# First pair's operands in a fixed order, and weights handled in pairs of blocks

## The chip, the core and the metric

The kernel runs on one core of one Trainium2 chip, as one program. The metric is device time in microseconds, the median of several runs. One execution more is taken by the hardware profiler; the views below are of that one. Engines are named as the profile names them: PE is TensorE (PEld its weight loads), DVE VectorE, ACT ScalarE, POOL GpSimd, SP the SyncE queue, which issues every DMA of this kernel.

## The reference

```python
q_bits = (einsum('bhsd,dk->bhsk', q, proj) > 0)          # 6 hash bits; k_bits likewise
mask = q_bucket[:, :, :, None] == k_bucket[:, :, None, :]
scores = where(mask, q @ k.T / sqrt(D), -1e9)
attn = exp(scores - max); attn = attn / (sum(attn) + 1e-9)
x = (attn @ v), heads side by side                       # [1536, 512]
h = maximum(x @ w_in1, 0); x = h * h @ w_out1
h = x @ w_in2; out = (maximum(h, 0) + alpha * minimum(h, 0)) @ w_out2
```

Batch 2, 8 heads, 768 positions, 64 columns a head; the feed-forward layers have 2048 hidden columns. Weights arrive as 64-bit floats and lie in memory as their bits, so the kernel itself has to turn them into 32-bit floats.

## The kernel before

**Tiling.** The 1536 rows are cut into four chunks of 384 (half a batch entry each). A chunk's attention goes by four pairs of heads (`Pair`), each pair with 2 x 3 score tiles of 128 x 768. A chunk's feed-forward pass goes by 16 blocks of 128 hidden columns: `hidden` multiplies x with a block of w_in, `project` the activated block with a block of w_out; the projection runs one block behind. Two layers of four chunks make eight passes of 16 blocks.

**Precision.** Every matmul operand is split into a high and a low half, both of the rounded type fp32r, and products are summed from several matmuls. For scores the halves, and rows that encode the hash ids, are stacked in 128 rows: q1 and k1, q2 and k2. So each pair has to be prepared: hash bits (`hash_bits`: a small matmul, then a sign on DVE), a match matmul with a constant code (`matches`), high and low halves, and id rows. For all pairs but the first, halves and id rows are computed for both heads in one instruction and moved to their place by DMA (`k_split`, `k_ids`, `q_split`, `q_ids`: 14 moves a pair, all on SP). The first pair computes its pieces in place, each head for itself; its queries come by a load of their own (`qr`).

**Weights.** `load_bits` loads a block's bits (512 KB), `to_f32` converts it (one ACT copy with a scale into the tile `we`, three DVE operations with the scratch tile `wsg`), `ahead` and `fetch` store the float block to memory for later passes (256 KB), and `split_w` makes the high half on ACT and the low half on POOL or DVE. All of it is done block by block, 512 columns an instruction. In passes 1 and 2 of the first layer the second layer's 32 blocks are converted beside the other work (`conversion`, a load and a conversion for each block as two steps).

**Order.** Chunk 0's attention runs alone. Then each feed-forward pass of the first layer carries the next chunk's attention in its slots: a `Background` runs the attention's steps by marks in time. A planner in the language's layer orders the instructions of each engine by priority and its own picture of time, except for instructions given to `keep_in_program_order`, which stay in the order of the program among themselves. In the kernel before these are the constants on DVE (L150 to L168) and the first pair's two sign instructions (L235). Every engine works its list strictly in order, and SP its DMA issues too. `prepare` gives the steps of a pair's preparation; one of them is put behind each score tile of the pair before, from its second tile on, and the raw loads of the next pair are the last step (`ahead`).

**Buffers.** Raw keys and queries have two buffers (`p2`); before the handover a weight block has four buffers (`whole`), its bits three (`wide`), its halves two; `we` and `wsg` have one each.

## Time and profile before

| | us |
|---|---|
| median of 3 runs | 852.25 (851.3 to 853.84) |
| the profiled execution | 850.58 |
| its span, first to last instruction | 848.8 |
| first matmul of the first feed-forward pass | 86.49 |

| engine | busy us | share of the span |
|---|---|---|
| PE | 798.8 | 94% |
| PEld | 648.0 | 76% |
| DVE | 504.0 | 59% |
| ACT | 470.5 | 55% |
| POOL | 359.6 | 42% |

A busy time is the union of an engine's instructions in the profile. Matmuls overlap and their ends are modelled, so a busy PE may still have small holes. A wait is put down to the instruction whose semaphore came last. The idle time of an engine that nobody waits for costs nothing.

### The profile page before, as it was taken

Reading aid. Unit: us, or ns where it says so; the run is one execution under the profiler, and the core shown is the slowest. Engines: PE = TensorE matmul, PEld = TensorE weight load, DVE = VectorE, ACT = ScalarE, POOL = GpSimd, SP = SyncE. Lnnn points to the kernel's source line nnn. Section 1 sums busy time; section 2 is a strip of 40 time slices with the busy share of each in tenths; the row PEclk is TensorE's granted clock in tenths of the full one; section 3 lists DMA queues with packets and bytes.
Section 4 is the critical chain, followed back from the end, with each engine's and each line's share of the span. In section 5 each row is a group of like instructions: output and inputs, shape, how many; then the busy total and the mean of one; then the engine's idle time right before and its main releaser. Section 6 shows DMA issues by size and latency. Waiting matters only on the chain.

```text
span 848.8 us, 12785 instructions
## 1 busy us (share of the span) xinstructions
PE 798.8 (94%) x4384; PEld 648.0 (76%) x4384; DVE 504.0 (59%) x819; ACT 470.5 (55%) x919; POOL 359.6 (42%) x315
## 2 busy tenths in 40 slices
PE   3988799999999989999989999999999999999997
PEld 1656486767787666677677789989989998998996
DVE  6576789998567567788888431224435445444442
ACT  3566587777575655565565556654434443444332
POOL 1000232323555565533333355545555555555553
PEclk9999799999999999999999999999999999999999
DMA  7567767777867767778775489600101011000001
GB/s 206 153 174 214 226 229 249 239 252 249 228 215 215 236 192 240 234 245 257 241 219 170 120 310 314 233 29 10 38 1 37 1 38 38 1 1 37 1 1 38
DMA packets 62096, 130.09 MB, mean 153 GB/s; under 512 B 8816, under 2 KB 21072, under 8 KB 62032
## 3 DMA queue, kind: packets, MB, share of 16 engines
q1 hardware_dynamic: 62032, 129.28, 48.6%
q8 instruction: 35, 0.57, 0.3%
q14 instruction: 29, 0.24, 0.1%
HBM read 83.32 MB, written 23.12 MB: 125 GB/s over the span
## 4 chain that ended last, share of the span: by engine, by line
PE 48%; DVE 7%; DMA 3%; issue 2%; ACT 2%; POOL 1%; SPq 0%; POOLq 0%; DVEq 0%; ACTq 0%
PE acc L608 7%; PE acc L604 7%; PE acc L605 7%; PE m L578 4%; PE m L576 4%; PE m L577 4%; PE h L576 3%; PE h L577 3%; PE h L578 3%; PE m L387 3%; DMA w<-we 2%; DVE low L354 1%; DVE wsg L504 1%; DVE we L507 1%; DVE pt L377 1%
## 5 line engine op out<-in xcount | busy, mean ns | idle before, releaser
L594 POOL TENSOR_TENSOR gl<-g,gh 128x384 fp32r<-128x384 f32 x128 | 136.1, 1063 | 246.0 <-ACT gh L593 123.2
L604 PE MATMUL acc<-wh,gh 128*128 128x512 f32 x384 | 158.2, 412 | 0.0
L529 POOL TENSOR_TENSOR wl<-wf,wh 128x512 fp32r<-128x512 f32 x80 | 108.4, 1356 | 112.8 <-ACT wh L528 102.5
L605 PE MATMUL acc<-wl,gh 128*128 128x512 f32 x384 | 152.1, 396 | 0.0
L528 ACT ACTIVATE wh<-w 128x512 fp32r<-128x512 f32 x128 | 80.5, 629 | 80.8 <-PE m L577 45.6
L608 PE MATMUL acc<-wh,gl 128*128 128x512 f32 x384 | 115.8, 398 | 2.1 <-POOL gl L594 2.1
L528 ACT ACTIVATE wh<-wf 128x512 fp32r<-128x512 f32 x128 | 80.5, 630 | 64.8 <-PE h L577 24.2
L576 PE MATMUL h<-xh,wh 128*128 128x384 f32 x296 | 106.7, 360 | 4.6 <-ACT xh L415 3.2
L354 DVE TENSOR_REDUCE low<-s 128x1 f32<-128x768 f32 x84 | 80.1, 953 | 38.0 <-PE s L351 37.8
L577 PE MATMUL h<-xl,wh 128*128 128x384 f32 x296 | 101.6, 343 | 0.4 <-POOL xl L416 0.4
L578 PE MATMUL h<-xh,wl 128*128 128x384 f32 x296 | 101.5, 343 | 0.0
L357 ACT ACTIVATE sm<-s,low 128x768 f32<-128x768 f32 x84 | 75.6, 900 | 37.5 <-DVE low L354 37.1
L608 PEld LDWEIGHTS acc<-wh,gl 128*128 128x128 f32 x384 | 71.5, 188 | 21.3 <-POOL gl L594 5.0
L371 PE MATMUL m<-ident,sm 128*128 128x128 f32 x525 | 82.9, 276 | 4.0 <-ACT sm L357 1.8
L529 POOL TENSOR_TENSOR wl<-w,wh 128x512 fp32r<-128x512 f32 x64 | 82.7, 1291 | 6.0 <-ACT wh L528 6.0
L604 PEld LDWEIGHTS acc<-wh,gh 128*128 128x128 f32 x384 | 72.4, 189 | 15.9 <-issue 5.7
L605 PEld LDWEIGHTS acc<-wl,gh 128*128 128x128 f32 x384 | 72.5, 189 | 9.2 <-issue 0.6
L593 ACT ACTIVATE gh<-g 128x384 fp32r<-128x384 f32 x64 | 33.5, 524 | 81.7 <-DVE g L592 81.7
L591 DVE TENSOR_SCALAR r<-m,alpha_sb 128x384 f32<-128x384 f32 x43 | 26.6, 618 | 87.0 <-PE m L578 86.7
L371 PEld LDWEIGHTS m<-ident,sm 128*128 128x128 f32 x525 | 64.1, 141 | 18.5 <-ACT sm L357 3.0
L350 PE MATMUL s<-k,q 128*128 128x384 f32 x168 | 63.9, 380 | 12.6 <-ACT sm L357 10.6
L578 PE MATMUL m<-xh,wl 128*128 128x384 f32 x216 | 73.0, 338 | 0.5 <-DVE wl L529 0.5
(112 smaller groups left out, 1475.2 us busy)
## 6 DMA issues: line engine op xcount, KB each, us to landing
wf<-w SPq DMA_DIRECT2D x96, 256.0 KB
wbits<-in_w_in_dram SPq DMA_DIRECT2D x32, 512.0 KB
wbits<-in_w_out_dram SPq DMA_DIRECT2D x32, 512.0 KB
w<-wf SPq DMA_DIRECT2D x32, 256.0 KB
w<-we SPq DMA_DIRECT2D x32, 256.0 KB
w<-w SPq DMA_DIRECT2D x32, 256.0 KB
q<-qh SPq DMA_DIRECT2D x60, 96.0 KB
k<-kh SPq DMA_DIRECT2D x28, 192.0 KB
```

The costliest lines, as they stand in the source:

```text
L354: nc.vector.tensor_reduce(low, ps[:, 0:2, 0:HALF], AX.XY, ALU.max, negate=True)
L357: nc.scalar.activation(sm.rearrange("p (a n) -> p a n", a=2), ps[:, 0:2, 0:HALF], AF.Exp, bias=low, accum_out=self.sums[:, i:i + 1],)
L371: nc.tensor.transpose(ps[:, i * P:(i + 1) * P], pp[:, b * P:(b + 1) * P], ident)
L528: nc.scalar.activation(hi, w, AF.Copy)
L529: engine.tensor_tensor(lo, w, f32(hi), ALU.subtract)
L576: nc.tensor.matmul(hp, wih[:, ks], xh[:, kk, :], start=first, stop=False)
L577: nc.tensor.matmul(hp, wih[:, ks], xl[:, kk, :], start=False, stop=False)
L578: nc.tensor.matmul(hp, wil[:, ks], xh[:, kk, :], start=False, stop=last)
L594: nc.gpsimd.tensor_tensor(gl, g, f32(gh), ALU.subtract)
L604: nc.tensor.matmul(acc[:, t, :], gh[:, blocks[t]], woh, start=first, stop=False)
L605: nc.tensor.matmul(acc[:, t, :], gh[:, blocks[t]], wol, start=False, stop=False)
L608: nc.tensor.matmul(acc[:, t, :], gl[:, blocks[t]], woh, start=False, stop=last)
```

## The change

The first pair gets a routine of its own, `at_once`, in which the DVE operations, the hash matmuls and signs stand in a written order (`self.next` is `keep_in_program_order` for the first two pairs of chunk 0). Two of its pieces are copied by POOL and two moved by DMA; the extra load `qr` goes. A pair's raw loads are issued by the first preparation step of the pair before, across chunks too, and in chunk 0 two preparation steps stand behind a score tile, from the first tile on. The low half of the queries is written over the raw ones.

A block of w_out and the next block of w_in are now a unit: one tile of 2 x 512 columns is loaded, converted, stored, fetched and split together, with one ACT instruction of 1024 columns for the high half and three DVE instructions of 1024 columns for a conversion. The ACT step of the conversion writes over the bits, and the tile `we` is gone: what `ahead` converts is left in `wsg` and stored from there. Low halves stay one instruction a block. `split(i)` stands once at the head of block i (before: w_in of block i + 1 and w_out of block i as two splits), `fetch` reaches one block ahead (before: two). `whole` and `wide` have two buffers of a pair each before the handover, eight after it. The rest of the diff saves a few small tiles among the constants.

```diff
+        def next(self, ins):
+            if self.c == 0 and self.j < 2:
+                tc.keep_in_program_order(ins)
...
+        def at_once(self):
+            self.start()
+            self.new_k()
+            self.new_q()
+            r = [self.rows(h)[0] for h in range(2)]
+            o = [self.rows(h)[1] for h in range(2)]
+            k_bits = self.hash_bits(self.kr, S)
+            for h in range(2):
+                nc.scalar.activation(self.k1[r[h], h], self.kr[r[h]], AF.Copy)
+            for h in range(2):
+                nc.scalar.activation(self.q1[r[h], h], self.qn[r[h]], AF.Copy, scale=scale)
+            nc.gpsimd.tensor_copy(self.k2[r[0], 0], f32(self.k1[r[0], 0]))
+            nc.gpsimd.tensor_copy(self.q1[o[0], 0], f32(self.q1[r[0], 0]))
+            nc.sync.dma_start(out=f32(self.k2[r[1], 1]), in_=f32(self.k1[r[1], 1]))
+            nc.sync.dma_start(out=f32(self.q1[o[1], 1]), in_=f32(self.q1[r[1], 1]))
+            k_y = self.matches(k_bits, S)
+            for h in range(2):
+                self.next(nc.vector.tensor_tensor(
+                    self.k1[o[h], h], self.kr[r[h]], f32(self.k1[r[h], h]), ALU.subtract
+                ))
+                if h == 0:
+                    q_y = self.matches(self.hash_bits(self.qn, T), T)
+                    for g in range(2):
+                        nc.scalar.activation(self.q2[o[g], g], q_y[o[g], 0, :], AF.Relu, bias=off[o[g]])
+                self.next(nc.vector.tensor_scalar(
+                    self.k2[o[h], h].rearrange("p (a n) -> p a n", n=T), k_y[o[h]], pop[o[h]], NEG,
+                    ALU.not_equal, ALU.mult,
+                ))
+                self.next(nc.vector.scalar_tensor_tensor(
+                    self.q2[r[h], h], self.qn[r[h]], scale, f32(self.q1[r[h], h]), ALU.mult, ALU.subtract
+                ))
...
             def ahead():
-                if self.j + 1 < NPAIR:
-                    load_pair(self.c, self.j + 1)
+                c, j = divmod(self.c * NPAIR + self.j + 1, NPAIR)
+                if c < NCH:
+                    load_pair(c, j)
             def first():
+                ahead()
                 self.start()
...
+            if self.first:
+                return [self.at_once, ahead]
+            if self.c % 2:
+                return [first, self.q_ids]
+            return [first, self.k_split, self.k_ids, self.q_split, self.q_ids]
...
-                if nxt and u > 0:
-                    steps.append(nxt.pop(0))
+                for _ in range(2 if c == 0 else 1):
+                    if nxt:
+                        steps.append(nxt.pop(0))
...
+    def to_f32(us, w=None):
+        if us not in w_bits:
+            load_bits(us)
+        n = len(us)
+        t = w_bits.pop(us)
+        e = t[:, 0:n, :, 1]
+        nc.scalar.activation(e.bitcast(F32), e.bitcast(F32), AF.Copy, scale=2.0 ** -112)
+        s = state["conv"].tile([P, 2, DM], U32, tag="wsg", name="wsg")[:, 0:n]
+        nc.vector.tensor_scalar(s, e, 0x80000000, None, ALU.bitwise_and)
+        nc.vector.scalar_tensor_tensor(s, t[:, 0:n, :, 0], 29, s, ALU.logical_shift_right, ALU.bitwise_or)
+        w = s if w is None else w.bitcast(U32)
+        nc.vector.scalar_tensor_tensor(w, e, 3, s, ALU.logical_shift_left, ALU.bitwise_or)
+        return w.bitcast(F32)
+
+    def ahead(us):
+        store(us, to_f32(us))
...
+    def blocks_of(i):
+        u = []
+        if 0 <= i:
+            u.append((work[i][0], work[i][2], 1))
+        if i + 1 < len(work):
+            u.append((work[i + 1][0], work[i + 1][2], 0))
+        return tuple(u)
...
+    def split(i):
+        us = blocks_of(i)
+        w, parts = w_f.pop(i)
+        hi = state["parts"].tile([P, 2, DM], F32R, tag="wh", name="wh")
+        lo = state["parts"].tile([P, 2, DM], F32R, tag="wl", name="wl")
+        if parts is None:
+            nc.scalar.activation(hi, w, AF.Copy)
+            parts = [w[:, 0], w[:, 1]]
+        else:
+            for k, p in enumerate(parts):
+                nc.scalar.activation(hi[:, k], p, AF.Copy)
+        for k, u in reversed(list(enumerate(us))):
+            engine = nc.gpsimd if u[2] or i // KFF == 1 else nc.vector
+            engine.tensor_tensor(lo[:, k], parts[k], f32(hi[:, k]), ALU.subtract)
+            w_split[u] = (hi[:, k], lo[:, k])
...
-            split(i + 1, 0)
-            split(i, 1)
+            split(i)
             g = hidden(l, c, f, x, step)
-            fetch(i + 2)
-            for u in units(i + 3):
-                if u not in w_d and u[0] == 0:
-                    load_bits(u)
+            if i + 1 < len(work):
+                fetch(i + 1)
+            if i + 2 < len(work) and bits_of(i + 2) and state["attention"]:
+                load_bits(bits_of(i + 2))
...
-        for o in range(2):
-            steps += [lambda u=(1, f, o): load_bits(u), lambda u=(1, f, o): ahead(u)]
+        us = ((1, f, 0), (1, f, 1))
+        steps += [lambda us=us: load_bits(us), lambda us=us: ahead(us)]
```

## Rows read from the trace of the kernel before

**Rows 1.** Stretches: length, busy us (instructions) of PE, PEld, DVE, ACT, POOL; clock, DMA, GB/s

```profile
0.00:18.90 18.90, 6.08 (x38) 3.44 (x39) 11.46 (x32) 6.21 (x8) 3.76 (x11) 1.00 0.72 206
18.90:86.50 67.60, 59.40 (x375) 39.83 (x374) 45.14 (x76) 44.70 (x98) 3.03 (x3) 1.00 0.64 182
86.50:110.00 23.50, 17.87 (x90) 12.71 (x91) 16.73 (x27) 12.96 (x25) 5.89 (x6) 0.78 0.75 241
110.00:498.00 388.00, 372.57 (x2157) 284.83 (x2156) 291.97 (x456) 247.35 (x500) 165.03 (x136) 1.00 0.72 225
415.00:445.00 30.00, 28.12 (x162) 20.87 (x160) 22.68 (x37) 17.54 (x36) 8.96 (x8) 1.00 0.77 233
498.00:848.80 350.80, 342.87 (x1730) 307.23 (x1728) 138.73 (x231) 159.28 (x289) 181.86 (x160) 1.00 0.17 60
```

**Rows 2.** Timeline of the start, first pair: start us, length us, engine, line, operation

```profile
1.04 0.13 POOL L146 IOTA part<- 128x8 int32 x1
...
3.75 1.71 ACT L259 ACTIVATE k<-kr 64x768 fp32r<-64x768 f32 x2 [1.74 <-DMA kr<-in_kT_dram]
...
4.63 2.45 DVE L260 TENSOR_TENSOR k<-kr,k 64x768 fp32r<-64x768 f32 x2 [4.63 <-ACT k L259]
...
7.11 0.69 DVE L150 CAST of<-part 128x8 f32<-128x8 int32 x1
...
12.33 0.35 DVE L235 TENSOR_SCALAR bits<-m 128x192 bf16<-128x192 f32 x1
...
12.73 0.80 PE L249 MATMUL s<-bits,code 128*128 128x192 bf16 x4 [4.11 <-DVE bits L235]
...
13.57 2.05 DVE L280 TENSOR_SCALAR k<-s,pop 64x768 fp32r<-64x768 f32 x2 [0.43 <-PE s L249]
...
16.81 1.18 ACT L311 ACTIVATE q<-h,off 64x384 fp32r<-64x384 f32 x2 [5.69 <-PE h L249]
...
18.86 0.96 DVE L354 TENSOR_REDUCE low<-acc 128x1 f32<-128x768 f32 x1 [1.70 <-PE acc L351]
```

**Rows 3.** Timeline of the start, preparation of the second pair

```profile
9.87 0.84 ACT L264 ACTIVATE kh<-kr 128x768 fp32r<-128x768 f32 x1 [1.98 <-DMA kr<-in_kT_dram]
...
10.62 0.51 ACT L317 ACTIVATE qh<-qn 128x384 fp32r<-128x384 f32 x1
...
12.60 0.55 DVE L318 SCALAR_TENSOR_TENSOR ql<-qn,qh 128x384 fp32r<-128x384 f32 x1
...
15.71 0.94 DVE L265 TENSOR_TENSOR kr<-kr,kh 128x768 fp32r<-128x768 f32 x1
```

**Rows 4.** Timeline, first exponential of the third and of the fourth pair

```profile
52.48 0.90 ACT L357 ACTIVATE sm<-acc,low 128x768 f32<-128x768 f32 x1 [2.22 <-DVE low L354]
...
69.35 0.59 SPq L324 DMA_DIRECT2D q<-qy  x1
...
74.38 0.90 ACT L357 ACTIVATE sm<-s,low 128x768 f32<-128x768 f32 x1 [4.71 <-DVE low L354]
```

**Rows 5.** Timeline, handover from attention to the first feed-forward pass

```profile
97.13 0.55 DVE L414 TENSOR_TENSOR x<-u,rb 128x384 f32<-128x384 f32 x1
...
98.29 0.69 PE L576 MATMUL h<-xh,wh 128*128 128x384 f32 x1 [3.20 <-ACT xh L415]
```

**Rows 6.** Chain that ended last, 405 to 445 us: start us, length us, what

```profile
417.55 4.34 DMA w<-we
...
435.57 4.03 DMA w<-we
```

**Rows 7.** Waits: engine and line, for whom, us in total, times, longest

```profile
ACT we L502 <- DMA w<-we: 16.6, 10, 3.9
...
SPq L554 <- POOL wl L529: 50.0, 33, 3.5
```

**Rows 8.** Scratch tile of the conversion: ns min/median/max, first and last start

```profile
L504 DVE TENSOR_SCALAR wsg<-wbits x64: 383/427/1510, 56.9 to 465.4; 128x512 uint32<-128x512 uint32 x64
...
L507 DVE SCALAR_TENSOR_TENSOR we<-we,wsg x32: 668/692/1719, 213.8 to 472.3; 128x512 uint32<-128x512 uint32 x32
```

More of the change, by code (lines that the diff above doesn't have):

```diff
@@ L77 @@
     m2 = pool("m2", 2)
-    state_whole = pool("whole", 4)
+    state_whole = pool("whole", 2)
     weights = ctx.enter_context(ExitStack())
@@ L142, in constants @@
             of = once.tile([P, 2 * NG], F32, name="of")
-            sign = once.tile([P, D], F32, name="sign")
+            sign = cols.bitcast(F32)
             nc.gpsimd.iota(row, [[0, 1]], base=0, channel_multiplier=1)
@@ L188, in load_pair @@
         nc.sync.dma_start(out=qn, in_=qT[b, h0:h0 + 2, :, s0:s0 + T].rearrange("h d s -> (h d) s"))
-        qr = None
-        if c == 0 and j == 0:
-            qr = p1.tile([P, 2, T], F32, tag="kh", name="qr")
-            for r in range(2):
-                nc.sync.dma_start(
-                    out=qr[r * D:(r + 1) * D], in_=qT[b, h0:h0 + 2, :, s0:s0 + T].rearrange("h d s -> d h s")
-                )
         if c % 2 == 0:
@@ L230, in hash_bits @@
             for g in range(NG):
-                nc.tensor.matmul(
+                self.next(nc.tensor.matmul(
                     ps[g * GR:(g + 1) * GR, 0:w], proj_sb.rearrange("p h n -> p (h n)"), x[:, g * w:(g + 1) * w],
                     start=True, stop=True,
-                )
-            ins = nc.vector.tensor_scalar(bits, ps[:, 0:w], 0.0, None, ALU.is_gt)
-            if self.first:
-                tc.keep_in_program_order(ins)
+                ))
+            self.next(nc.vector.tensor_scalar(bits, ps[:, 0:w], 0.0, None, ALU.is_gt))
             return bits
@@ L276, in k_ids @@
             y = self.matches(self.bits, S)
-            if self.first:
-                for h in range(2):
-                    r, o = self.rows(h)
-                    nc.vector.tensor_scalar(
-                        self.k2[o, h].rearrange("p (a n) -> p a n", n=T), y[o], pop[o], NEG,
-                        ALU.not_equal, ALU.mult,
-                    )
-                return
             kn = p1.tile([P, S], F32R, tag="kn", name="kn")
@@ L486 @@
     kept = {}
+    here = {}
     y_d = {}
[L489 to L510 removed]
@@ new lines, in store, with keep @@
+    def store(us, w):
+        for k, u in enumerate(us):
+            w_d[u] = dram.tile([P, DM], F32, tag="w%d_%d_%d" % u, name="w%d_%d_%d" % u)
+            nc.sync.dma_start(out=w_d[u], in_=w[:, k])
+    def ahead(us):
+        store(us, to_f32(us))
+    def keep(u):
+        l, f, o = u
+        g = f if o else (f - 1) % KFF
+        if g not in kept:
+            kept[g] = state["res"].tile([P, 2, DM], F32, name=f"w{g}")
+        nc.sync.dma_start(out=kept[g][:, 1 - o], in_=w_d[u])
+        here[u] = kept[g][:, 1 - o]
@@ L562, in split, with bits_of @@
-    def split(i, o):
-        for u in units(i)[o:o + 1]:
-            split_w(u, nc.gpsimd if o or i // KFF == 1 else nc.vector)
+    def blocks_of(i):
[5 more added lines that the diff above has]
+        return tuple(u)
+    def bits_of(i):
+        return tuple(u for u in blocks_of(i) if u not in w_d and u not in here)
+    def fetch(i):
+        us = blocks_of(i)
+        if all(u in here for u in us):
+            if len(us) == 2:
+                w_f[i] = (kept[us[0][1]], None)
+            else:
+                w_f[i] = (None, [here[us[0]]])
+            return
+        ring = "whole" if state["attention"] else "wide"
+        w = state[ring].tile([P, 2, DM], F32, tag=ring, name="wf")
+        new = bits_of(i)
+        if len(new) == 2:
+            to_f32(us, w)
+            store(us, w)
+        else:
+            for k, u in enumerate(us):
+                if u in new:
+                    to_f32((u,), w[:, k:k + 1])
+                    store((u,), w[:, k:k + 1])
+                elif u in w_d and u not in here:
+                    nc.sync.dma_start(out=w[:, k], in_=w_d[u])
+        w_f[i] = (w, None) if len(us) == 2 and not any(u in here for u in us) else (
+            None, [here[u] if u in here else w[:, k] for k, u in enumerate(us)]
+        )
@@ L692 @@
         step()
+    fetch(-1)
     fetch(0)
-    fetch(1)
-    split(0, 0)
+    split(-1)
     state["moe"] = True
```

123 lines of the change are left out of this document (29 added, 94 removed).

## The prediction, made before the change was timed

> **What bounds the kernel now.** I read the table of stretches first [rows 1]. The reader is to see five stretches of different kind. Up to 18.9 us TensorE is busy for 6.08 us: nothing has a score yet. From 18.9 to 86.5 us the attention of chunk 0 runs alone, and TensorE is idle for 8.2 of 67.6 us. From 86.5 to 110 us the first feed-forward pass takes over, with 5.6 us idle and a granted clock of 0.78, so part of it at 1.2 GHz. From 110 to 498 us feed-forward and attention are woven together, and TensorE is idle for 15.4 of 388 us. From 498 us on it is busy for 342.87 of 350.8 us with one kind of work. So a change can win at the start, a little in the woven stretch, and next to nothing in the last 350 us, however much ScalarE and VectorE time it saves there.
>
> Then the timeline of the start [rows 2]. VectorE does nothing until 4.63 us, when it takes the subtraction of the first keys, and begins the constants only at 7.11, though their input from GpSimd (L146) is there at 1.17. The sign bits of the keys need the constants' engine and come at 12.33, the match matmuls at 12.73, the id rows at 13.57, the query's id rows at 16.81, the first row maximum (L354) at 18.86. The chain of the first 18.9 us is VectorE's order of work, not a transfer.
>
> **The change part by part.**
>
> *First pair in a fixed order.* The constants now lead on VectorE. Before they took 7.11 to 12.33 = 5.2 us, with two query subtractions among them; from 1.2 us on they end at 6.4 at the latest. Then, in the written order, with durations of [rows 2] and [rows 3]: key bits 0.35 (6.8); match matmuls 0.80 (7.6), beside which the first low half of the keys runs, 2.45 / 2 = 1.2 (8.0); query bits, taken as another 0.35 (8.4); id rows of one head 2.05 / 2 = 1.0 (9.4); query low half 0.55 (10.0). ScalarE's id rows of the query, 1.18 for both heads, lie beside the last two. Before, the first maximum followed the first head's last id row (16.81 + 1.18 / 2 = 17.40) by 1.46; so now it comes near 11.4. The second head takes 1.2 + 1.0 + 0.55 = 2.8 more on VectorE, to 12.8, before its scores are due. 18.86 - 11.4 = 7.5 us gained. Bounds: 9 if the constants really need only the 4.1 us that are left without the two subtractions and their gaps, 4 if the scheduler puts the second head's three pieces ahead of the first maximum and the move of the queries (two DMAs replace two GpSimd and ScalarE pieces) lands late. The two new moves wait on SP for ScalarE's copies (L259 ends at 5.46, two of the queries at 0.51 follow), and the load of the second pair may queue behind them until about 6.5; the holes of the start no longer hang on it, and its scores are due only after six of the first pair.
>
> *What the idle start had hidden.* Until 18.86 the second pair's preparation ran in the holes: on ScalarE 0.84 + 0.51, on VectorE 0.55 + 0.94 [rows 3]. With a shorter start it falls beside scores. 1.5 us of VectorE if all of it shows, nothing if it finds holes; I take +1.0.
>
> *Loads two pairs ahead, two preparation steps to a score.* At the start of a pair ScalarE stands until the first maximum: 2.22 us for the third pair, 4.71 us for the fourth [rows 4]. The fourth pair's last operand move is issued at 69.35, its first exponential comes at 74.38. The excess, 4.71 - 2.22 = 2.5 us, is what late operands cost; I take -2.5 (bounds 0 and -4.7). What is late next is the second product of the pair before, which stands ahead of the scores on TensorE. Later chunks have 32 us per pair (388 for 12), and their loads were early already: 0.
>
> *Handover at 86.5.* The feed-forward waits for the last pair's x: its product is queued on VectorE until 97.13, and TensorE stands 3.20 us for it [rows 5]. The edit leaves this chain (sums, a round trip through memory, one multiplication) as it is; only what stands ahead of it on VectorE differs: conversions of 1024 columns. 0, with bounds of -4 and +7 (rival below). The Trainium skill ("TensorE: Matmul & The Clock Gate", "HAM oscillation") says that an idle TensorE falls to the half clock until it has been busy again. The trace agrees: 0.78 in this stretch is (1 - 0.78) x 2 x 23.5 = 10.3 us at 1.2 GHz. By that rule a handover without the hole would give back up to half of these, about 5 us (sum 834); since no edit shortens the chain I leave it out.
>
> *Weights in pairs.* ScalarE, from 384 columns at 0.51 and 768 at 0.84 [rows 3]: 0.86 ns per column, so 1024 cost 1.06 against 2 x 0.62 by the same slope; 0.2 us less per pair. VectorE, two inputs, 0.55 and 0.94: 1024 cost 1.2 against 2 x 0.68. So 10 to 15 us less VectorE work and some 25 us less ScalarE work in the whole run. ScalarE now also writes its conversion back into every second word, which no row shows: at worst 2 x 1.06. None of this is on TensorE's path after 498 us: the split of a pair of blocks may start when the projection two back has ended and is due one block later, about 4.4 us (350.8 us for the last 80 blocks), and needs 1.06 on ScalarE, 0.68 on VectorE, and the GpSimd subtraction that every block has today as well. So 0 there, bounds -1 and +2.
>
> In the woven stretch two waits go. ScalarE waited 16.6 us in 10 pieces for the store of converted weights, and SP 50.0 us in 33 pieces for a weight buffer that GpSimd still read [rows 7]; now the store's source is the VectorE scratch, and a fetch goes into a buffer read one block earlier. But the price of such waits is low: three of them stand in the chain between 415 and 445 us, the first of 4.34 and the last of 4.03 us [rows 6], and in that stretch TensorE is idle for only 1.88 of 30 us [rows 1]: 1.88 / 12.6 = 0.15 of the wait. 16.6 x 0.15 = 2.5 us, and 0.5 for fewer instructions: -3. Bounds: -11 (most of the 15.4 idle) and +10 (next rivals).
>
> The Trainium skill ("SBUF — State Buffer", "Who interferes with whom") says that VectorE and GpSimd lock each other out of a shared port for a whole instruction. The trace bears it out: the sign mask (L504) takes 0.427 us at the median and 1.510 at most, 1.08 more [rows 8]. By the rule 32 fewer masks are spared at most 32 x 1.08 = 35 us of VectorE time, at 0.15 some 5 us (sum 834); the median says that most were never blocked.
>
> **Sum.** -7.5 + 1.0 - 2.5 + 0 - 3 = -12. The profiled execution took 850.58 us (span 848.8), so 838.6; the median of the runs, 852.25, is 1.7 above it, and I predict 840.
>
> **The rivals.**
>
> 1. *The handover takes it back.* One conversion of 1024 columns (0.8 + 1.2 + 1.2 = 3.2 us) in front of x's product lengthens the hole of 3.20 to 6.4; the low clock, 10.3 us now, holds 8 longer, and at half the rate that costs 4; the preparation shows in full (+0.5). -12 + 3.2 + 4 + 0.5 = -4.3: 848. For it: VectorE is 71% busy there; against: conversions come half as often.
> 2. *The woven stretch clears.* If the exponentials behind ScalarE's waits were what delayed the scores, 11 of the 15.4 us idle go: 840 - 8 = 832, down to 826. For it: DMA waits stand in the chain; against: 0.15 above.
> 3. *Slower: VectorE takes over the store's wait.* The converted pair lies in the single scratch buffer, so the next mask, on VectorE, waits for both stores to land, up to 2 x 4.34 = 8.7 us, and everything behind it on VectorE (row maxima, copies of transposes) with it. 32 blocks of the second layer were finished between 213.8 and 472.3 us [rows 8], so 16 pairs stand 16.2 us apart on average, and there is no wait if they are spread. At 16 full waits, 139 us x 0.15 = 21, dearer if VectorE hides less than ScalarE did: -9 + 21 = +12, 864; with half of them standing, at 0.25, +8: 860. It decides against the change once VectorE waits more than some 60 us in all, 3.7 us a pair, that is when conversions follow each other within 5 us.
> 4. *The order does not take hold.* If the scheduler still puts the constants late, the start keeps its 18.9 us: 840 + 6.5 = 846.5. VectorE's instructions are all bound by the order, so I give it little.
>
> **Chances.** A measurement of this kernel can tell 0.3% (2.6 us) from no change. Forecast 0.53 (833 to 846, all faster but 0.02), rival 1 0.13 (half faster, half the same), rival 2 0.14 (faster), rival 3 0.16 (slower), rival 4 0.04 (faster, a part the same). Faster 0.74, same 0.10, slower 0.16. The range 826 to 854 leaves out the far half of rival 3 and the tail of rival 2; the forecast's own is 833 to 846.
>
> **What would show it.** The constants on VectorE before 2 us and the first row maximum near 11; the first feed-forward matmul near 77 instead of 86.5; ScalarE without a wait for a store; VectorE's waits for stores near zero between 214 and 472 us; the last stretch of 350 us within 2 us. Wrong, if the first hidden matmul is not earlier by 6 us or more, if the hole before x's product grows past 6 us, or if masks wait for stores again and again.

## The result, and the profile after

The changed kernel takes 862.45 us against 853.02 for the kernel before on the same chip: ratio 1.012 [1.009, 1.015], 9.4 us slower, where 840 was predicted. One execution of it took 4375.86 us, with a mean of 1423 ns for a hidden matmul of 128x384 where the profile below has 358; it is left out and its cause stays open. The profile below is of another execution of the same kernel (run e1_after, 860.21 us, span 858.1).

The stretches (columns as in [rows 1]); the limits are the first row maximum, the first hidden matmul, 110 us, and the first matmul of pass 3 (498 us before, 503.7 now):

```profile
0.00:11.40 11.40, 5.68 (x37) 3.06 (x38) 8.98 (x29) 5.16 (x7) 2.06 (x11) 1.00 0.81 245
11.40:84.20 72.80, 60.57 (x376) 40.62 (x375) 47.94 (x78) 47.05 (x101) 4.28 (x4) 0.95 0.69 197
84.20:110.00 25.80, 23.32 (x130) 17.89 (x131) 15.94 (x22) 15.92 (x30) 6.25 (x6) 0.87 0.75 229
110.00:503.70 393.70, 369.51 (x2117) 282.80 (x2116) 281.36 (x369) 234.01 (x416) 170.95 (x135) 1.00 0.68 217
503.70:858.10 354.40, 344.49 (x1729) 306.59 (x1727) 150.02 (x231) 150.26 (x211) 223.29 (x160) 1.00 0.17 60
```

The first maximum comes 7.5 us earlier, the first hidden matmul only 2.3 (86.5 before). From 110 us on, both halves of the kernel are longer: TensorE is idle for 24.2 us in the woven stretch instead of 15.4, and the last part takes 354.4 us instead of 350.7, although ScalarE has fewer instructions in both and VectorE fewer in the first (as many as before in the last). GpSimd is busy for 223.3 us in the last part, 181.9 before.

The start of the changed kernel (timeline as in [rows 2]), and the second pair's first maximum in the kernel before:

```profile
1.21 0.17 DVE L148 CAST of<-part 128x8 f32<-128x8 int32 x1 [1.21 <-POOL part L144]
...
11.39 0.96 DVE L361 TENSOR_REDUCE low<-acc 128x1 f32<-128x768 f32 x1
...
15.04 0.65 ACT L515 ACTIVATE wbits<-wbits 128x512 f32<-128x512 f32 x1 [5.93 <-DMA wbits<-in_w_in_dram]
15.59 0.88 ACT L364 ACTIVATE sm<-acc,low 128x768 f32<-128x768 f32 x1
...
16.47 0.83 ACT L258 ACTIVATE kh<-kr 128x768 fp32r<-128x768 f32 x1
...
34.49 0.96 DVE L361 TENSOR_REDUCE low<-s 128x1 f32<-128x768 f32 x1 [1.29 <-PE s L358]
```

```profile
35.53 0.96 DVE L354 TENSOR_REDUCE low<-s 128x1 f32<-128x768 f32 x1 [0.52 <-PE s L351]
```

The first exponential (L364) could follow the maximum at 12.4. It stands behind a conversion of weights (L515), which the planner has drawn into the idle start and which waits 5.93 us for its load; in the kernel before, the first conversion's mask ran only at 56.9 us [rows 8]. The copy of the second pair's keys (L258), at 9.87 before [rows 3], stands behind both. So the second pair's first maximum comes at 34.49, one microsecond earlier than before (35.53). TensorE meanwhile (stretches of 4 us; length, PE busy, clock, DMA share, GB/s):

```profile
8.00:12.00 4.00, 3.10 (x14) 1.00 0.99 304
12.00:16.00 4.00, 0.57 (x2) 1.00 1.00 381
16.00:20.00 4.00, 3.38 (x20) 0.51 0.86 276
20.00:24.00 4.00, 4.00 (x22) 0.63 0.91 217
```

The granted clock is at 2.4 GHz while TensorE is busy for 0.57 of 4 us, and at 1.2 GHz for most of the next 8. The Trainium skill ("TensorE: Matmul & The Clock Gate", "HAM oscillation") says that an idle TensorE drops to the half clock until it has been busy again; the rows from 12 us on agree. Against the kernel before this is no loss, although its column reads 1.00 up to 86.5 us [rows 1]: the profiles hold no clock record before 12.7 us here and 24.5 us there, and the column shows 1.00 where there is none. The same matmul of 128x384 tells the level: 0.52 us at the half clock, 0.33 to 0.34 at the full one. First the kernel before, then the changed one (TensorE's timeline):

```profile
23.94 0.52 PE L351 MATMUL s<-k,q 128*128 128x384 f32 x1
...
24.57 0.33 PE L351 MATMUL s<-k,q 128*128 128x384 f32 x1
```

```profile
21.92 0.52 PE L358 MATMUL acc<-k,q 128*128 128x384 f32 x1
...
23.48 0.34 PE L358 MATMUL s<-k,q 128*128 128x384 f32 x1
```

Both kernels run their first scores at 1.2 GHz. By the clock records the changed one is at 2.4 GHz for good from 22.9 us on, the one before from 24.5, until the handover.

Behind the start, the wait that the earlier loads were to remove has moved. ScalarE's waits from 20 to 84 us, first before, then changed (as in [rows 7]; `low` is the row maximum, `h` of L387 and L394 the second product, `u` its copy):

```profile
ACT sm L357 <- DVE low L354: 14.6, 7, 4.7
...
ACT u L393 <- PE h L387: 1.9, 2, 1.6
```

```profile
ACT u L400 <- PE h L394: 8.6, 2, 4.9
...
ACT sm L364 <- DVE low L361: 1.1, 2, 0.8
```

ScalarE no longer waits for row maxima, but for the second product of the pair before, which stands ahead of them on TensorE.

Waits of the changed kernel from 110 to 503.7 us (as in [rows 7]):

```profile
ACT wbits L515 <- DMA wbits<-in_w_out_dram: 10.3, 7, 3.5
...
PEld h L610 <- POOL wl L595: 4.8, 4, 2.2
...
ACT wbits L515 <- DMA wbits<-in_w_in_dram: 3.7, 4, 1.3
...
PE h L610 <- POOL wl L595: 3.4, 3, 1.9
...
DVE wsg L517 <- DMA w<-wsg: 1.5, 3, 0.9
```

ScalarE's 16.6 us for stores [rows 7] are gone, and 14.0 us for the load of the bits stand in their place. VectorE waits 1.5 us for stores in three waits. New is TensorE's wait for low halves that GpSimd makes.

### The profile page after: what moved, and what is told of

Its sections match the earlier page's. It is cut to its first block, busy times and chain, and to the rows that moved or that the text cites. A ratio compares the mean times of both kernels' runs of the same rounds, so it can differ in the third digit from the quotient of the medians.

```text
span 4373.9 us, 12383 instructions
## 1 busy us (share of the span) xinstructions
PE 4356.8 (100%) x4384; PEld 3164.7 (72%) x4384; DVE 484.7 (11%) x726; ACT 459.7 (11%) x763; POOL 385.6 (9%) x315
## 4 chain that ended last, share of the span: by engine, by line
PE 100%; ACT 0%; DMA 0%; DVE 0%; issue 0%; SPq 0%; ACTq 0%
PE acc L636 12%; PE acc L637 12%; PE acc L640 12%; PE m L378 8%; PE m L394 8%; PE h L608 7%; PE h L609 7%; PE h L610 7%; PE m L610 5%; PE m L608 5%; PE m L609 5%; PE s L357 4%; PE s L358 4%; PE h L394 1%; PE s L711 1%; PE h L378 1%
## 5 line engine op out<-in xcount | busy, mean ns | idle before, releaser
L636 PE MATMUL acc<-wh,gh 128*128 128x512 f32 x384 | 680.3, 1772 | 0.0
L637 PE MATMUL acc<-wl,gh 128*128 128x512 f32 x384 | 653.0, 1701 | 0.0
L640 PE MATMUL acc<-wh,gl 128*128 128x512 f32 x384 | 565.3, 1698 | 0.0
L608 PE MATMUL h<-xh,wh 128*128 128x384 f32 x296 | 421.1, 1423 | 0.6 <-ACT r L616 0.6
L609 PE MATMUL h<-xl,wh 128*128 128x384 f32 x296 | 408.9, 1382 | 0.0
L610 PE MATMUL h<-xh,wl 128*128 128x384 f32 x296 | 408.5, 1380 | 0.0
L378 PE MATMUL m<-ident,sm 128*128 128x128 f32 x531 | 403.0, 1048 | 0.7 <-DVE pt L384 0.7
L394 PE MATMUL m<-pt,vr 128*64 128x384 f32 x336 | 354.1, 2334 | 0.4 <-DVE rrow L410 0.4
L608 PE MATMUL m<-xh,wh 128*128 128x384 f32 x216 | 296.1, 1371 | 0.0
L357 PE MATMUL s<-k,q 128*128 128x384 f32 x168 | 237.4, 1413 | 3.0 <-ACT sm L364 3.0
L358 PE MATMUL s<-k,q 128*128 128x384 f32 x168 | 230.3, 1371 | 0.0
L394 PEld LDWEIGHTS m<-pt,vr 128*64 128x64 f32 x336 | 76.6, 461 | 209.2 <-issue 197.5
```

Source lines behind the costliest of these rows:

```text
L357: nc.tensor.matmul(ps[:, a, 0:HALF], self.q1[:, h, qs], self.k1[:, h, ks], start=True, stop=False)
L358: nc.tensor.matmul(ps[:, a, 0:HALF], self.q2[:, h, qs], self.k2[:, h, ks], start=False, stop=True)
L378: nc.tensor.transpose(ps[:, i * P:(i + 1) * P], pp[:, b * P:(b + 1) * P], ident)
L394: nc.tensor.matmul(self.o[r, 0:T], self.vr[:, b, r], self.pt[h][:, :, b, :], start=(b == 0), stop=(b == NKB - 1),)
L608: nc.tensor.matmul(hp, wih[:, ks], xh[:, kk, :], start=first, stop=False)
L609: nc.tensor.matmul(hp, wih[:, ks], xl[:, kk, :], start=False, stop=False)
```

## The experiments

All kernels run the same matmuls. To see where a kernel gains or loses, each matmul was given a fixed weight for its kind, and the time at which a kernel reaches a sum of weights was compared with that of before (profiled executions; minus is ahead). "120" is the sum that before reaches at 125 us, some blocks behind the handover, "500" the one at 500 us. Last part: from pass 3's first matmul to the end. Executions of one kernel differ by 4.5 to 8.5 us on one chip (before, on all chips: 847.8 to 856.9), so one profile's lead is good to a few us. The ratios rest on 5 to 12 executions of a run and 17 to 26 of before on the same chip. The runs were made on several chips, where before has medians of 850.99 to 851.85; so runs are best compared by their ratios. The row "before" has the median beside e1 to e3.

| run | median us | ratio to before | lead at 120 | lead at 500 | lost between | last part |
|---|---|---|---|---|---|---|
| before | 851.06 | | | | | 350.7 |
| e1_after | 860.90 | 1.0114 [1.0088, 1.0140] | -5.4 | +5.6 | 11.0 | 354.4 |
| e2_first_only | 849.63 | 0.9984 [0.9970, 0.9999] | -5.5 | +1.1 | 6.6 | 350.3 |
| e3_pairs_only | 859.83 | 1.0096 [1.0068, 1.0125] | -2.2 | +4.2 | 6.4 | 356.1 |
| e4_low_on_vector | 860.05 | 1.0087 [1.0056, 1.0119] | -5.2 | +4.2 | 9.4 | 356.4 |
| e5_split_by_block | 854.96 | 1.0026 [1.0005, 1.0046] | -4.2 | +4.7 | 8.9 | 350.3 |
| e6_convert_by_block | 859.48 | 1.0081 [1.0052, 1.0110] | -6.6 | +1.3 | 7.9 | 354.3 |
| e7_first_chunk_only | 851.19 | 0.9980 [0.9962, 0.9998] | -4.3 | +2.6 | 6.9 | 350.4 |
| e8_first_weights_held | 849.29 | 0.9980 [0.9966, 0.9995] | -5.4 | -1.0 | 4.4 | 350.3 |
| e9_three_part_buffers | 857.97 | 1.0079 [1.0057, 1.0101] | -7.3 | +2.1 | 9.4 | 353.9 |
| e10_mended | 859.44 | 1.0091 [1.0064, 1.0118] | -7.7 | +11.2 | 18.9 | 350.3 |
| e11_split_convert_by_block | 852.47 | 1.0017 [1.0000, 1.0034] | -2.8 | +2.8 | 5.6 | 350.3 |
| e12_two_copies | 860.45 | 1.0116 [1.0095, 1.0138] | -6.9 | +12.4 | 19.3 | 351.0 |
| e13_longer_start | 855.58 | 1.0052 [1.0033, 1.0070] | -1.6 | +5.5 | 7.1 | 350.3 |
| e14a_lead_82 | 855.75 | 1.0054 [1.0033, 1.0076] | -1.0 | +4.0 | 5.0 | 350.4 |
| e14b_lead_78 | 857.20 | 1.0068 [1.0050, 1.0085] | +0.6 | +8.5 | 7.9 | 350.4 |
| e16_order_pinned | 852.12 | 1.0013 [0.9998, 1.0028] | -0.9 | +1.1 | 2.0 | 350.7 |
| e17_longer_start_pinned | 852.50 | 1.0022 [1.0005, 1.0039] | +1.7 | +2.0 | 0.3 | 350.2 |
| e18_order_pinned_later | 850.77 | 0.9989 [0.9972, 1.0005] | -7.8 | +1.0 | 8.8 | 350.3 |

### Which part costs

The changed kernel again, without an edit:

> The changed kernel itself, since its one profiled execution so far was disturbed. Time 860 to 863. Three theories of where the 9 us more come from. Handover (rival 1): first row maximum near 11 and 5 to 10 us saved up to the last product of chunk 0, but the hole before the first feed-forward block grows from 3.2 to over 6 us and the stretch up to the end of that handover is no shorter than before. Store's wait (rival 3): VectorE's sign masks wait over 60 us in all for the stores out of the scratch tile, and the woven stretch (388 us before) grows by 15 us or more. Less slack (new): nobody waits for stores, but TensorE waits for the halves of the weights, which now come from one fetch a block ahead and one split; over 10 us of waits of TensorE for wh and wl.

The first part alone (first pair, raw loads, two preparation steps to a score): every edit of the weights undone, for instance

```diff
-            split(i)
+            split(i + 1, 0)
+            split(i, 1)
```

> The first part alone: first pair in its fixed order, raw loads earlier, two preparation steps a score; weights block by block as before. If the start's gain is real and kept: 842 to 846 (7 to 10 us faster). If the fixed order harms the pairs that follow, or the handover takes the gain back whatever the weights do: 850 to 856.

The weights alone: the attention as before, but with the low half of the queries over the raw ones, which makes room:

```diff
-            if self.first:
-                return [self.at_once, ahead]
...
+                if nxt and u > 0:
+                    steps.append(nxt.pop(0))
```

> Weights in pairs alone, the first pair as before (to make room, the low half of the queries is written over the raw ones and some small constants share tiles). If the pairs cost what the whole change lost beside a start that gained: 866 to 874. If pairs are harmless and the first part is to blame: 848 to 854. Store's wait theory: waits of VectorE for the stores over 60 us; handover theory: the hole before x's product over 6 us, woven stretch as before.

The first part gains at most 0.3%, the weights in pairs cost 1.0%. So the result is a loss of the weights; the 7.5 us by which the first maximum comes earlier have nearly all gone too. By the profiles the changed kernel is 5.4 us ahead behind the handover, and loses 11.0 in the woven passes and 4.0 behind them.

### The last part: one copy, two low halves

```diff
+    def split(i, o):
...
+            if u[2] != o:
+                continue
+            hi = state["parts%d" % o].tile([P, DM], F32R, tag=f"wh{o}", name=f"wh{o}")
+            lo = state["parts%d" % o].tile([P, DM], F32R, tag=f"wl{o}", name=f"wl{o}")
+            nc.scalar.activation(hi, parts[k], AF.Copy)
...
+            engine.tensor_tensor(lo, parts[k], f32(hi), ALU.subtract)
```

> The changed kernel, but the high halves are made block by block again (two ScalarE copies of 512 columns, w_in of the next block first, own buffers for the two kinds of block, three for w_in in the last part); loading, conversion, storing and fetching stay in pairs. Theory B: with one ScalarE copy of 1024 columns VectorE's and GpSimd's low halves are released at the same moment and lock each other out (GpSimd's low half 1.80 us at the median instead of 1.29), and this and the two buffers cost the 3.7 us by which the last part (from pass 3 on) became longer: now that part takes 350 to 351.5 us instead of 354.4, GpSimd's low half 1.3 us, and the kernel 856 to 858. Rival C: the last part is longer because a fetch reaches only one block ahead; then it stays at 354, and the kernel at 860.

```diff
-        state["parts"] = pool(f"parts{late}", 2, stack)
+        state["parts"] = pool(f"parts{late}", 2 + late, stack)
```

> The changed kernel with three buffers instead of two for the halves of a pair of blocks in the last part (from pass 3 on). Since the halves by block brought the last part from 354.4 back to 350.3 us, this asks which side of it did so. Theory B1: ScalarE's copy waits for the projection that still reads the buffer (64 waits, 24.1 us in all); with a third buffer it is a block earlier, and the last part takes 350 to 351.5 us, the kernel 857. Theory B2: the two low halves that one copy releases together lock each other out whatever the buffers; GpSimd's low half stays at 1.8 us, its gl at the pass ends stays late, the last part 353 to 354.5, the kernel 860.

```diff
-            nc.scalar.activation(hi, w, AF.Copy)
...
+        for k, p in reversed(list(enumerate(parts))):
+            nc.scalar.activation(hi[:, k], p, AF.Copy)
```

> The changed kernel, but the high halves of a pair of blocks are made by two ScalarE copies of 512 columns, w_in of the next block first, into the same common buffer of a pair. Theory B2: the last part is longer because one copy of 1024 columns releases both low halves at once, 0.4 us later than the first of two copies would, and they lock each other out; then it takes 350 to 352 us instead of 354.4, and the kernel 856 to 858. Rival B1: it is the common buffer, which the copy may only overwrite when the projection has ended; then 353.5 to 354.5, and the kernel 860 or more.

The halves by block bring the last part back to 350.3 us; a third buffer does not (353.9); two copies into the common buffer do (351.0). So theory B2 holds for the last part, and B1 and C fall. For the whole kernel B2's 856 to 858 us did not come: the two copies took 860.45 (1.0116, as the changed kernel), since 19.3 us were lost in the passes before. The halves by block took the ratio from 1.0114 to 1.0026, more than the last part's 4.1 us, and the passes have a part in that too. GpSimd's low half in the last part, first the kernel before, then the changed one, the third buffer, and two copies (busy us, mean ns | idle before):

```profile
L529 POOL TENSOR_TENSOR wl<-w,wh 128x512 fp32r<-128x512 f32 x64 | 82.7, 1291 | 6.0 <-ACT wh L528 6.0
```

```profile
L595 POOL TENSOR_TENSOR wl<-w,wh 128x512 fp32r<-128x512 f32 x64 | 112.6, 1759 | 33.3 <-ACT wh L588 32.6 <-POOL gl L626 0.7
```

```profile
L595 POOL TENSOR_TENSOR wl<-w,wh 128x512 fp32r<-128x512 f32 x64 | 111.7, 1745 | 31.4 <-ACT wh L588 31.4
```

```profile
L593 POOL TENSOR_TENSOR wl<-w,wh 128x512 fp32r<-128x512 f32 x64 | 83.3, 1302 | 45.7 <-POOL gl L624 24.0 <-ACT wh L590 21.6
```

And the end of pass 4 in the changed kernel (timeline):

```profile
642.65 1.00 POOL L626 TENSOR_TENSOR gl<-g,gh 128x384 fp32r<-128x384 f32 x1 [1.03 <-ACT gh L625]
642.88 1.06 ACT L588 ACTIVATE wh<-w 128x1024 fp32r<-128x1024 f32 x1 [0.31 <-PE acc L640]
...
643.71 0.50 PE L640 MATMUL acc<-wh,gl 128*128 128x512 f32 x1 [0.35 <-POOL gl L626]
643.97 0.69 DVE L595 TENSOR_TENSOR wl<-w,wh 128x512 fp32r<-128x512 f32 x1 [1.96 <-ACT wh L588]
644.01 1.80 POOL L595 TENSOR_TENSOR wl<-w,wh 128x512 fp32r<-128x512 f32 x1 [0.36 <-ACT wh L588]
```

The copy ends at 643.94, VectorE and GpSimd start 0.04 us apart, and GpSimd takes 1.80 us: about its own 1.29 and a good part of VectorE's 0.69. The Trainium skill ("SBUF — State Buffer", "Who interferes with whom") names the port that these two share as an exclusive lock; here that costs 0.47 us in the mean of 64 low halves, and with two copies, which let VectorE go first, it is gone. In the last part TensorE's waits for wl, wh and gl are 4.8 us in the changed kernel, 2.6 before and 3.1 with two copies. So the profile shows 2.2 of the 3.7 us as waits; the rest appears only in the length of the part.

### The woven stretch: low halves and conversions

```diff
-            engine = nc.gpsimd if u[2] or i // KFF == 1 else nc.vector
+            engine = nc.gpsimd if u[2] else nc.vector
```

> The changed kernel, but in pass 1 too the low half of the w_in block is made by VectorE; GpSimd keeps the low half of the w_out block alone. Theory A: in pass 1 (228.6 to 379.3 us) TensorE stands for the second of two low halves that GpSimd makes one behind the other (8.2 us of waits of a hidden matmul for it between 110 and 500 us), so pass 1 gets 4 to 6 us shorter and the kernel comes to about 856. Rival: these waits only take the place of others and VectorE, which gets 16 operations of 0.69 us more, delays row maxima instead: 860 to 863, pass 1 within 2 us of 150.7.

```diff
+        for k in range(n):
+            e = t[:, k, :, 1]
+            nc.scalar.activation(e.bitcast(F32), e.bitcast(F32), AF.Copy, scale=2.0 ** -112)
+            nc.vector.tensor_scalar(s[:, k], e, 0x80000000, None, ALU.bitwise_and)
...
```

> The changed kernel, but a pair of blocks is converted in instructions of 512 columns (two ScalarE, six VectorE instead of one and three), loaded, stored, fetched and split in pairs as before. Theory D: the VectorE operations of 0.69 and 1.23 us stand ahead of row maxima and hash bits, and this is the 4 us of the woven stretch that the pairs lose beyond pass 1: passes 0 to 2 take 415 us instead of 419.5, the kernel about 857. Rival: the three VectorE operations of a pair follow each other in any case, so the delay is the same or, with six instructions, larger: 860 to 863.

The next run has both edits, halves and conversions by block.

> The changed kernel with the halves and the conversions block by block; what stays of the pairs is that two blocks are loaded, stored and fetched together and that a fetch reaches one block ahead instead of two. With the halves alone by block the ratio to the kernel before was 1.0026, where the first part by itself gives 0.998. Theory D2: the rest, about 4 us, is VectorE operations of 0.69 and 1.23 us in front of row maxima and hash bits; then it is now about 851. Rival H: it is the shorter reach of the fetches and the buffers of pairs; then it stays at 854 to 856.

Neither edit alone is told apart from the changed kernel by its interval. Theory A falls: pass 1 is 148.8 us instead of 150.8, and waits of TensorE for exponentials take the place of those for low halves (14.7 us for L364 from 110 to 500 us, 11.6 in the changed kernel). Theory D gets some support from a wait, none from a ratio: with conversions by block TensorE hardly waits for GpSimd's low halves in the woven stretch. First the run with halves by block but conversions in pairs, then the one with both by block (110 to 500 us):

```profile
PEld h L610 <- POOL wl L595: 6.6, 5, 2.9
PE h L610 <- POOL wl L595: 5.0, 5, 2.5
...
PE acc L637 <- POOL wl L595: 2.6, 3, 1.7
```

```profile
PE h L613 <- POOL wl L598: 0.6, 1, 0.6
PE acc L640 <- POOL wl L598: 0.5, 1, 0.5
```

7.6 us of TensorE's waits (the lines with PE) against 1.1, for 0.8 us in the ratios (1.0026 and 1.0017, intervals that overlap).

A hole in these passes can cost more than its length. The granted clock of a stretch of 10 us reads 0.83 in the changed kernel from 365 to 375 us, and in the run with two copies from 235, 280, 355 and 475 us on; in the kernel before it stays at 2.4 GHz from 110 us to the end of the passes. 0.83 is (1 - 0.83) x 2 x 10 = 3.4 us at 1.2 GHz, up to 1.7 us lost each time.

### Where the start's gain goes

```diff
             def first():
-                ahead()
+                if self.c == 0:
+                    ahead()
...
-                    if nxt:
+                    if nxt and (c == 0 or u > 0):
```

> The kernel before with the first part of the change in chunk 0 alone: from chunk 1 on a pair's raw loads are its predecessor's last preparation step again, and preparation begins behind the second score tile, as in the kernel before. With the whole first part the kernel was 6 us ahead at equal TensorE work from 104 to 215 us and had lost it by 280 us. Theory E: the earlier loads and preparation of the later chunks put hash and match matmuls ahead of operands that are not there (holes of 1.71 us for hash bits at 216.6 us, of 0.77 us for the id rows at 234.6); then the lead stays and the kernel takes 843 to 845. Rival F: the lead is lost whatever the order of the later preparation, since pass 1 has a pace of its own: 848 to 850.

In the next two runs `state["moved"]` is the last operand move of chunk 0's third pair; the second of them also has the halves by block.

```diff
-    fetch(0)
-    fetch(1)
+    with tc.issue_after(state["moved"]):
+        fetch(0)
+        fetch(1)
```

> The kernel before with the first part of the change, and the loads of the first weight blocks held behind the operand moves of chunk 0's third pair. With the first part alone the first row maximum came at 11.4 us, but the first exponential only at 15.65, behind a conversion of weights (56.8 us in the kernel before, now 15.07) that waited 5.8 us for its load; the second pair's first row maximum came at 34.6 (35.5 before). Theory G: this conversion, drawn into the idle start, is what takes the gain of the start; held back, the first exponential comes at 12.4, the second pair's first maximum at 28 to 31, and if the woven passes keep the lead the kernel takes 844 to 846. Rival: the second pair's moves and not the weights set its start (maximum at 33 or later): 849. Rival F again: the start becomes 4 us shorter, but the woven passes give it back: 848 to 850.

```diff
+    with tc.issue_after(state["moved"]):
+        fetch(-1)
+        fetch(0)
+    split(-1, 0)
```

> The changed kernel with the halves made block by block and the first weights' loads held as in the run with the first part: both known losses of the change undone, the pairs of loads, conversions, stores and fetches kept. By theories B and G together 850 to 852 (855 with the halves by block alone, less 4). If the hold is worth nothing, 855.

Theory E falls (0.998, as with the whole first part). Holding the weights does in the start what theory G says (timeline of that run, then two matmuls of TensorE's):

```profile
12.49 0.90 ACT L367 ACTIVATE sm<-acc,low 128x768 f32<-128x768 f32 x1 [3.28 <-DVE low L364]
...
13.38 0.83 ACT L259 ACTIVATE kh<-kr 128x768 fp32r<-128x768 f32 x1
...
31.36 0.96 DVE L364 TENSOR_REDUCE low<-s 128x1 f32<-128x768 f32 x1 [4.24 <-PE s L361]
```

```profile
16.25 0.52 PE L361 MATMUL s<-k,q 128*128 128x384 f32 x1
...
18.72 0.34 PE L361 MATMUL acc<-k,q 128*128 128x384 f32 x1
```

The exponential comes 3.1 us earlier than in the changed kernel, the second pair's maximum too, and TensorE is at 2.4 GHz by 18.7 us; but the time is not mended: 0.998 again, with a lead at 120 of 5.4 us against 5.5 without the hold. So the first weights cost the start its gain for a while, and not the kernel its time. And the mended form of the whole change, expected at 850 to 852, took 859.44: its last part is 350.3 us, but it loses 18.9 us in the passes. Its ratio is 1.0091, that of the halves by block without the hold 1.0026; an edit that mends the start made this kernel slower.

### Order alone

```diff
+            pad = once.tile([P, DM], F32, name="pad")
+            first(nc.vector.memset(pad, 0.0))
+            for _ in range(8):
+                first(nc.vector.tensor_tensor(pad, pad, pad, ALU.add))
```

> The kernel before with nine operations of 512 columns that do nothing needed, on VectorE ahead of the constants: the first row maximum comes at 21 to 24 us instead of 18.9. Theory F (the woven passes have a pace of their own and absorb what the start gains or loses): the kernel stays within 1.5 us of the kernel before. Rival (a lost microsecond of the start stays lost, only a gained one is taken back by a new order): 2 to 5 us slower.

```diff
-LEAD = 0.8
+LEAD = 0.82
```

> The kernel before with LEAD 0.82 instead of 0.8: the attention of a chunk is spread over a little more of the pass before it. No operation is added or taken away, only the order of the woven work changes. Theory I: the order of the kernel before is a favourable one, and any other costs 2 to 8 us in passes 0 to 2 (411.6 us), pass 1 above all: 854 to 859. Rival: the order matters little, within 1.5 us of the kernel before.

```diff
-LEAD = 0.8
+LEAD = 0.78
```

> The kernel before with LEAD 0.78 instead of 0.8, the other direction, again with no operation more or less. Theory I: 2 to 8 us slower than the kernel before, as with 0.82. Rival J: not the order as such but the closeness of the attention's end to the pass's end sets it; then 0.82 and 0.78 lie on opposite sides of the kernel before.

LEAD 0.82 costs 0.54% and LEAD 0.78 costs 0.68%, that is 4.6 and 5.8 us of 851, on both sides of 0.8 and with not one operation more: rival J falls, and theory I holds for these two orders (not that any other order costs as much, and not for pass 1 above all: it took 138.8 and 141.5 us, 141.2 before). The longer start (first maximum at 21.56) was level or ahead at the handover and lost its 7.1 us behind it. Theory F falls; the rival's 2 to 5 us came out, though not for its reason, since the lost start had been made up by then.

From the handover on, all instructions of an engine were then chained in the order that they have in the kernel before (`ORDER` holds the steps from one to the next, read off that kernel):

```diff
+    later = nc.cur_bb.bb.instructions[traced:]
+    for engine, order in ORDER.items():
...
+                tc.add_manual_dep(
+                    own[k], before.name,
+                    mybir.DependencyInfo(mybir.DependencyClass.NoSync, mybir.DependencyReason.DATA),
+                    reason="order",
+                )
```

> The first part in chunk 0 alone and the first weights held (the start as in the run with held weights, a tile of its own for the low half of the queries as before), and from the handover on every engine's instructions in the order that they have in the kernel before, given as a list. Theory I (the woven passes lose 5 to 7 us to their new order): the 6 us of lead at the handover stay, passes 0 to 2 as long as before, and the kernel takes 844 to 847. Rival (the passes have a pace of their own, or the old order does not fit an earlier start): 848 to 852.

> The kernel before with the nine needless operations ahead of the constants, and from the handover on the order of the kernel before, given as a list. With the planner's own order it was 4.5 us slower than the kernel before, although it was level at the handover. Theory I: without the new order the loss goes: within 2 us of the kernel before. Rival: it stays, 3 to 5 us slower.

With the old order the longer start loses 0.3 us instead of 7.1 behind the handover. The ratios, 1.0022 and 1.0052, are 2.6 us apart, and their intervals just overlap; so what it had lost was order, in the main. The early start loses 2.0 instead of 4.4, but its lead is gone by then, in one hole in the handover: a match matmul that the list puts early waits for hash bits (7.15 us).

```profile
97.09 0.50 PE L376 MATMUL m<-bits,code 128*128 128x96 bf16 x4 [7.15 <-DVE bits L364]
```

So the last run leaves the first 400 instructions behind the handover to the planner:

```diff
     later = nc.cur_bb.bb.instructions[traced:]
+    held_from = {id(i) for i in later[400:]}
...
+            if id(own[k]) not in held_from:
+                continue
```

> As the run with the pinned order and the held weights, but the first 400 instructions behind the handover (some four blocks of the feed-forward) are left to the planner, and the list holds only from there on. Theory I with the handover left free: the lead at the handover is 5 to 7 us as in the run with held weights, nothing of it is lost in the passes, and the kernel takes 844 to 847, faster than both kernels. Rival: the lead goes in the passes although the order is the old one, 849 to 852; then order alone is not the cause.

The lead is 7.8 us at 120 and is lost by 160 us, where the free and the listed order meet: TensorE stands for exponentials (rows below) and falls to the half clock (0.90 from 110 to 160 us). From there to the end it loses nothing more.

```profile
123.73 0.45 PE L495 MATMUL s<-k,q 128*128 128x384 f32 x1 [2.56 <-ACT sm L502]
...
126.90 0.69 PE L495 MATMUL s<-k,q 128*128 128x384 f32 x1 [1.40 <-ACT sm L502]
```

Neither of the two early starts got the 844 to 847 of theory I; both came out at the rival's figure (852.12 and 850.77), so order alone is not shown to be what takes an early start's lead. Counted by the VectorE instructions that are still left, VectorE is only 3.4 us ahead of the kernel before at 90 us and 2.3 at 116, where TensorE is ahead by 8: TensorE had run ahead of the engine that feeds it. VectorE is busy for 292 of 388 us in the woven stretch before, with its fullest part right there (46.3 of 50 us from 110 to 160). Whether less VectorE work in pass 0 would keep the lead was not tried.

No run beats the kernel before by the 0.3% that the prediction set as what a measurement can tell; the nearest are the first part alone, in chunk 0 alone, and with the weights held, all at 0.998 with intervals that end just below 1.

## Why the prediction was wrong

The sum forecast a gain of 12 us; by the profiles it was a loss of 9.6. Two terms made the loss: the weights in the woven stretch, put at -3, cost 11.0, and the last part, put at 0, cost 3.7. The gain of the start was right, but little of it lasted.

- *First pair in a fixed order, -7.5*: right. Constants from 1.21 us, first maximum at 11.39 (11.4 predicted).
- *What the idle start had hidden, +1.0*: the first step that failed. It counted the second pair's preparation only. Another user of the hole, the first conversion of weights, took 3.2 us of the first exponential. But holding it back (e8) left the lead at 120 and the ratio as they were, so this is not where the 22 us between forecast and result come from.
- *Loads two pairs ahead, -2.5*: the wait went, the gain did not come. ScalarE's waits for row maxima from 20 to 84 us fell from 14.6 to 1.1 us, and its waits for the second product rose from 1.9 to 8.6. The prediction had named that product as late next, and put no time on it. At the sum that before reaches at 61 us the lead is 2.4 us, where 9 were predicted; and the first hidden matmul is 2.3 us earlier, where under 6 was named as a sign of being wrong.
- *Handover, 0*: the lead grows there from 2.4 to 5.4. The hole before x's product (3.20 us [rows 5]) did not grow: x is made at 90.89. The low clock holds (1 - 0.87) x 2 x 25.8 = 6.7 us instead of 10.3, where rival 1 had it 8 longer; rival 1 falls.
- *Weights in the woven stretch, -3*: the term that decided the result, wrong in sign: +11.0 from 120 to 500. Its price of waits, 0.15, is not tested by this: 16.6 us of ScalarE's went and 14.0 others came, and TensorE's idle time rose. (The three waits that it was read from add up to 12.86 us, not 12.6, as the middle one is 4.49; the 0.15 stays.) But no term stood for the order itself. The first part alone, with the weights as before, loses 6.6 of these us, where "later chunks" stood at 0. A change of LEAD, which does nothing else, loses 5.0 and 7.9 us there, and the old order takes nearly all of a longer start's 7.1 us away (e17). No run holds the order fixed for the changed kernel itself, so that order has this share in its 11.0 us is argued from these runs. What the pairs add, 11.0 - 6.6 = 4.4 us, stays open: GpSimd's low halves are a part of it by the waits, and no ratio shows it.
- *Last 350 us, 0 (bounds -1 and +2)*: +3.7. "One block later" was allowed 4.4 us, but one copy of 1.06 us releases two low halves on engines that share a port (e5, e12). The prediction had used that rule only for masks, as a possible gain; its cost stood in this step.
- *Rival 3*, the only slower one, had nearly the size (860 to 864) and not the mechanism: VectorE waited 1.5 us for stores, of some 60 needed. That its size fits is luck. Rivals 2 and 4 fall.

Together, by the profiles: 5.4 ahead at 120, 11.0 lost to 500, 4.0 more to the end: +9.6, with 860.21 against 850.58.

## What to carry to other kernels

Where a planner orders the engines, price the new order as well: nudge a constant that adds no work and see how far the time moves, before the gain of an edit is believed. A hole at the start is filled by whatever is ready, so ask what will be drawn into it and who then queues behind. When a wait goes, ask what stands next in line, and put a time on it. Joining two small instructions into one releases their two consumers at once; here these shared a port, and the join cost more than it saved.

## What was not expected of the hardware

- 512 columns of a two-input operation: GpSimd takes 1.29 us when its copy is its own, and 1.76 when VectorE's (0.69) starts with it (means of 64).
- The clock column can read 1.00 where the profile has no record: the first scores of the kernel before, the changed one and the one with held weights take 0.52 us a matmul there, and 0.34 at 2.4 GHz.
- Three weight loads of 512 KB and one of keys, issued at 8.8 to 10.3 us, hold a ScalarE instruction until 15.04; the DMA engines are at 1.00 and 381 GB/s from 12 to 16 us.
